# Cosine attention and a highway layer on one core: seven 64-key blocks with quadrant value products, one-piece value loads and stores, folded norm sums, a new order

## The chip, the core and the metric

The kernel runs on one core of one Trainium2 chip. A core has a matrix engine (TensorE, in profiles PE, with its weight loads listed apart as PEld), a vector engine (VectorE, DVE), an activation engine (ScalarE, ACT), a general engine (GpSimd, POOL) and a queue engine (SyncE, SP). SP, POOL and ACT issue the transfers, which 16 DMA engines carry out. TensorE multiplies a stationary operand by a moving one and adds into PSUM, eight banks of 512 float32 columns on 128 partitions. It can be used whole (128 x 128), as two column halves (128 x 64) or as four quadrants (64 x 64); a quadrant is given by the partition half that the operands come from and the partition half of PSUM that the result goes to.

The metric is the time of one execution on the device in microseconds; lower is better. Before the change three runs took 258.66 us (median), 256.27 and 260.71 us.

## What is computed

For 8 batches, 12 heads, 448 positions and 64 numbers per head, queries and keys are scaled to length one, scores are divided by tau = 0.1, and a softmax weights the values. The result, 3584 rows of 768, goes through a highway layer with two 768 x 768 matrices:

```python
q_n = q / (norm(q) + 1e-06);  k_n = k / (norm(k) + 1e-06)
scores = q_n @ k_n.T / tau
attn = exp(scores - max);  attn = attn / (sum(attn) + 1e-09)
x = (attn @ v)            # heads side by side: (3584, 768)
H = maximum(x @ w_h, 0);  T = 1 / (1 + exp(-(x @ w_t + b_t)))
out = T * H + (1 - T) * x
```

Since scores lie between -10 and 10, the kernel leaves the maximum out; the row sums come from a column of ones beside the values.

## The kernel before, in words

**Layout.** A head's 448 positions are split as 64 x 7: partition l holds positions 7l to 7l+6. "Block j" is the 64 positions with remainder j. Two heads of a pair (s = 0, 1) fill 128 partitions, and a group (b, g), i = 3b + g, has four heads: s = 0, 1 and t = 0, 1. There are 24 groups, three to a batch.

**Stages of a batch.** Loads: q on SP in float32, k and v on POOL, converted to 16 bits on the way. v comes in four transfers of 64 partitions (`ld_v`, L370), so that blocks 0 to 2 and 4 to 6, or 0 to 2 and 3 to 5, stand one above the other. `norm` (L402) squares 14 x 64 numbers (mostly ACT, L413; some on POOL or DVE, L415) and DVE sums each 64 of them (L421). A Newton iteration (L432 to L439; for batch 0 logarithm and exponential on ACT, L447 and L450) makes reciprocal lengths, `scale` (L462) multiplies on POOL or DVE, and `turn` puts the number index on the partitions: by PE with a copy out of PSUM on DVE (L474, L482) or by a transposing transfer on SP (L477).

**Attention, batches 1 to 6.** `scores` (L509) makes, for each head pair s, three tiles with 2 x 64 keys above each other for both t (two PSUM banks), and one more tile for the seventh block of all four heads. Every product is a quadrant product, 64 numbers by 64 keys by 448 queries (L316). ACT takes the exponential of each tile of 896 columns into `E` or `Et` (L521, L531), seven per group. `attend` (L535) works on one head pair after its four tiles: 24 full products of 128 keys x 128 queries by 65 value columns (L549) and 8 in column halves for the last 64 queries (L555). The seventh block is paired with zeros in `vp`, so that 128 keys can be used there too. All sums of a pair lie in one bank; DVE takes the reciprocal of the sums (L562) and multiplies (L563).

**Attention, batches 0 and 7.** `attend_tile` (L571) does the same for 128 queries at a time (the last tile 64), so that the highway layer can begin, or end, early (L606, L618, L620, L624, L638 to L643).

**Highway layer.** `ffn` (L648) turns x by a transposing transfer (L672) or PE (L668), multiplies by w_t and w_h (L692; L689 in column halves for the tile of 64 rows), adds the bias on DVE (L721), takes tanh on ACT (L734), makes the gate of it on DVE (L736), and finishes with L730, L757 and L762 (the last on POOL or DVE). The output leaves in two transfers per tile on SP, one per 64 rows (L769 for the short tile, L772 for the others).

**Order.** Every step is an entry ("op") with an engine. `ORDER` is one list of all 1684 ops, written out by hand or by a planner; each engine executes its own ops in that order, and `SLOTS` gives the buffer that each tile takes, among them the eight PSUM banks `B` (score tiles take two neighbouring ones). `ENGINE` moves single ops to another engine than their usual one. For the names in `PORT`, a POOL op is made to wait for the DVE op listed before it; transfers in `HELD` wait for the ACT op listed before them. 18 products on zeros (`wm`, L343) and 41 more (`wf`, L818) fill PE while it has nothing else.

Of the kernel before, what the change touches and what calls it, by code (L numbers as in the profile page):

```python
# [85 lines left out]

SLOTS = {
    "qr": "01010101",
    "kr": "0120121",
    "kn": "012012012120102120210210",  # L90
    "vr": "01010101",
    "vp": "01010101",
# [786 lines left out]
```

## Time and profile before

| | |
|---|---|
| three runs | 258.66 us median, 256.27 to 260.71 |
| the profiled execution: time / span from first to last instruction | 257.48 us / 255.7 us |
| granted TensorE clock | 0.996 of full |
| busy PE / DVE / ACT / POOL | 236.7 / 226.2 / 199.1 / 143.9 us |
| weight loads on PE | 150.0 us |
| DMA packets | 77241, 48.27 MB, 189 GB/s on average |

"Busy" is the union of an engine's instructions. PE's products overlap, and their ends are modelled, so that PE's busy time is more than it needs. Row labels give the line, the engine, the operation, what is written and read, the shape and the count; behind the bar stand the busy time of the group in microseconds, the mean duration of one in nanoseconds, and idle time ahead of it with what ended most of that. A timeline row gives start, length, and the instructions that it gathers. A wait row gives the engine and line that waited, the releaser, the total, the number of waits and the longest.

### The profile page before, as it was taken

What the parts mean: (1) busy time and instruction counts of PE and PEld (TensorE: products, weight loads), DVE (VectorE), ACT (ScalarE), POOL (GpSimd) and SP (SyncE); (2) the same over time, 40 slices, a digit from 0 to 9 for tenths busy, and PEclk for the clock granted to TensorE, in tenths of its full rate; (3) what the DMA queues carried; (4) which work ended last, traced back from release to release, by engine and by line L of the source; (5) the groups of instructions that cost most, each with busy time, mean ns of one, the idle gap of its engine ahead of it and who ended that gap; (6) DMA issues with size and microseconds to landing.
All of it is one profiled execution on the core that took longest, in us unless ns stands there. A gap on an engine that the chain in (4) does not pass through costs nothing.

```text
span 255.7 us, 8889 instructions
## 1 busy us (share of the span) xinstructions
PE 236.7 (93%) x3719; PEld 150.0 (59%) x3719; DVE 226.2 (88%) x509; ACT 199.1 (78%) x248; POOL 143.9 (56%) x172
## 2 busy tenths in 40 slices
PE   5997999999998799999989998899999999999990
PEld 2455675656765466656654654566665766667550
DVE  4869999999997999999997999898998997877894
ACT  3469998999998799999998987699887456875220
POOL 1964879889995769769269731166427221200610
PEclk9999999999999999999999999999999999999998
DMA  6999979999999999998899999999997966992645
GB/s 231 298 229 258 330 126 205 157 151 277 163 147 248 181 211 262 153 161 171 194 242 174 191 153 166 168 316 215 224 144 122 201 145 114 158 165 45 157 141 154
DMA packets 77241, 48.27 MB, mean 189 GB/s; under 512 B 52880, under 2 KB 74000, under 8 KB 77200
## 3 DMA queue, kind: packets, MB, share of 16 engines
q1 hardware_dynamic: 56912, 34.25, 63.2%
q0 software_dynamic: 19856, 12.68, 38.3%
q8 instruction: 29, 0.48, 0.8%
q10 hardware_dynamic: 432, 0.75, 0.8%
q14 instruction: 12, 0.10, 0.1%
HBM read 38.34 MB, written 11.01 MB: 193 GB/s over the span
## 4 chain that ended last, share of the span: by engine, by line
PE 50%; DVE 28%; DMA 9%; ACT 4%; issue 4%; POOL 3%; DVEq 0%; ACTq 0%; POOLq 0%
PE B L692 22%; PE B L316 8%; DMA xT<-x 6%; PE B L549 6%; DVE n L421 5%; PE B L818 3%; DVE hm L730 3%; DVE z L721 3%; DMA vr<-in_v_dram 3%; PE B L689 3%; PE B L343 3%; DVE x L563 2%; PE B L618 2%; ACT E L606 2%; DVE hm L757 2%
## 5 line engine op out<-in xcount | busy, mean ns | idle before, releaser
L521 ACT ACTIVATE E<-B 128x896 f16<-128x896 f32 x108 | 94.3, 923 | 13.8 <-PE B L316 9.5
L692 PEld LDWEIGHTS <-xT 128*128 128x128 f16 x576 | 51.9, 97 | 39.4 <-issue 7.3
L762 POOL TENSOR_TENSOR os<-x,hm 128x384 f32<-128x384 f16 x35 | 31.4, 912 | 56.1 <-DVE hm L757 14.2
L692 PE MATMUL B<-wt,xT 128*128 128x384 f16 x288 | 54.9, 326 | 2.2 <-DMA xT<-x 1.3
L692 PE MATMUL B<-wh,xT 128*128 128x384 f16 x288 | 54.7, 326 | 1.0 <-DMA xT<-x 0.8
L421 DVE TENSOR_REDUCE n<-sq 128x14 f32<-128x896 f32 (+1 forms) x50 | 50.8, 1037 | 2.7 <-ACT sq L413 2.7
L316 PE MATMUL B<-qT,kT 64*64 64x448 f16 (+2 forms) x1064 | 47.9, 283 | 3.5 <-DVE z L721 1.4
L606 ACT ACTIVATE E<-B 128x1024 f16<-128x1024 f32 (+2 forms) x42 | 36.2, 919 | 15.5 <-PE B L316 9.3
L462 POOL TENSOR_TENSOR qn<-qr,y 128x448 f16<-128x448 f32 x38 | 35.2, 936 | 21.0 <-PE B L689 4.1
L462 POOL TENSOR_TENSOR kn<-kr,y 128x448 f16<-128x448 f16 x33 | 30.4, 935 | 17.0 <-DMA kT<-kn 10.5
L549 PEld LDWEIGHTS <-E 128*128 128x128 f16 x648 | 30.4, 98 | 6.9 <-issue 3.6
L734 ACT ACTIVATE tt<-z 128x768 f16<-128x768 f32 (+1 forms) x32 | 24.4, 768 | 12.8 <-DVE z L721 12.7
L549 PE MATMUL B<-vp,E 128*128 128x65 f16 x648 | 33.9, 194 | 0.0
L316 PEld LDWEIGHTS <-kT 64*64 64x64 f16 x1064 | 20.6, 106 | 21.5 <-issue 15.0
L730 DVE SCALAR_TENSOR_TENSOR hm<-B,x 128x384 f16<-128x384 f32 x53 | 28.6, 548 | 4.0 <-PE B L692 2.9
L549 PE MATMUL B<-vp,Et 128*128 128x65 f16 x216 | 30.6, 194 | 0.0
L721 DVE TENSOR_TENSOR z<-B,bias 128x384 f32<-128x384 f32 x48 | 25.6, 549 | 0.9 <-PE B L692 0.5
L563 DVE SCALAR_TENSOR_TENSOR x<-B,rd 128x448 f16<-128x448 f32 x36 | 22.4, 621 | 0.9
L373 POOL DMA_DIRECT2D vr<-in_v_dram x32 | 21.7, 686 | 1.4 <-DVE vp L488 1.1
L549 PEld LDWEIGHTS <-Et 128*128 128x128 f16 x216 | 21.1, 98 | 0.0
L413 ACT ACTIVATE sq<-qr 128x896 f32<-128x896 f32 (+1 forms) x19 | 17.5, 942 | 2.8 <-DMA qr<-in_q_dram 2.8
L531 ACT ACTIVATE Et<-B 128x896 f16<-128x896 f32 x18 | 16.7, 926 | 0.5 <-PE B L316 0.4
(75 smaller groups left out, 307.0 us busy)
## 6 DMA issues: line engine op xcount, KB each, us to landing
out_dram<-os SPq DMA_DIRECT2D x47, 192.0 KB, 3.6
qr<-in_q_dram SPq DMA_DIRECT2D x6, 1344.0 KB, 7.7
kr<-in_k_dram POOLq DMA_DIRECT2D x7, 672.0 KB, 8.1
vr<-in_v_dram POOLq DMA_DIRECT2D x16, 192.0 KB, 6.6
qr<-in_q_dram SPq DMA_DIRECT2D x6, 448.0 KB, 5.8
vr<-in_v_dram POOLq DMA_DIRECT2D x16, 144.0 KB, 7.0
out_dram<-os SPq DMA_DIRECT2D x15, 96.0 KB, 3.5
wt<-in_moe_w_t_dram POOLq DMA_DIRECT2D x1, 1152.0 KB, 13.2
```

The costliest lines, as they stand in the source:

```text
L316: nc.tensor.matmul(out, lhsT=tokens("k", i, s, j, 1, ln), rhs=tokens("q", i, s, j0, n, ln), start=True, stop=True)
L421: nc.vector.reduce_sum(R("n2", b)[:, c : c + 7 * n], a, axis=AX.X)
L462: ENG[eng].tensor_mul(R(nm + "n", i)[:, :, t, :], source(nm, b, g)[:, t, :].rearrange("l (j d) -> l j d", d=D), R("y", b)[:, c : c + 7].un ...
L521: op("ACT", f"exd {n} {c}", lambda c=c, at=at, n=n: nc.scalar.activation(R("E", n)[:, 14 * c : 14 * c + 14, :].rearrange("l (t j) x -> l t ...
L549: nc.tensor.matmul(U_()[:, 2 * c + t, :], lhsT=keys(t, m, 2 * c, 2), rhs=values(b, g, s, t, m), start=(m == 0), stop=(m == NC))
L563: op("DVE", f"ev {n}", lambda: nc.vector.scalar_tensor_tensor(out=R("x", b)[:, :, D * p : D * p + D], in0=U_()[:, :, 0:D], scalar=0.0, in1 ...
L606: op("ACT", f"ex{m} {n}", lambda at_=at_, m=m, o=o: nc.scalar.activation(flat()[:, o : o + 2 * m].rearrange("l (t x) -> l t x", t=2), R2(a ...
L692: nc.tensor.matmul(P[:, 0:MH], lhsT=xT[:, cc, :], rhs=w_[:, cc, MH * mh : MH * mh + MH], start=(cc == 0), stop=(cc == CC - 1))
L721: op("DVE", f"za {g} {mh}", lambda at=at, sl=sl: nc.vector.tensor_add(R("z", g)[:, sl], R("B", at)[:, 0:MH], biast[:, :] if tail else bias ...
L730: op("DVE", f"hm {g} {mh}", lambda at=at, sl=sl, mh=mh: nc.vector.scalar_tensor_tensor(out=R("hm", g)[:, sl], in0=R("B", at)[:, 0:MH], sca ...
L734: op("ACT", f"th{nb} {g}", lambda: nc.scalar.activation(R("tt", g)[:, 0:W], R("z", g)[:, 0:W], AF.Tanh, scale=0.5), r=[("z", g), ("t0",)], ...
L762: op(eng, f"out {g} {mh}", lambda sl=sl, mh=mh, eng=eng: ENG[eng].tensor_add(R("os", g)[:, sl], xpart(mh), R("hm", g)[:, sl]), r=[("gg", g ...
```

## The change

- **Scores.** Each score tile now holds one 64-key block j of all four heads of a group: head pair s on the partition half s, t in the bank. Seven tiles of 896 columns as before; no tile of its own for a seventh block. `E` becomes 11 tiles of 1024 columns, `Et` goes.
- **Value products.** They use 64 keys and 64 queries each, in quadrants; part j of a group runs after exponential j and adds to sums of all four heads in a bank pair. 196 products per group. The zero padding of the values goes. One reciprocal (14 columns) and one multiplication (896 columns) finish a group.
- **Values.** One transfer per batch in k's layout; two copies per batch into `vp` (DVE, in three cases ACT and in one POOL); the separate copies of the seventh block go. The ones are set on POOL.
- **Norm sums.** For 42 of the 48 (q or k, batch, group) a fold first adds the upper 32 squares of each 64 to the lower 32, on POOL (23) or DVE (19); DVE then sums 32.
- **Stores.** One transfer per tile but for the last two tiles.
- **Engines.** 12 of the 32 gates move from DVE to ACT; of the 96 half-tile scalings 40 instead of 22 are on DVE, of the 53 output sums 30 instead of 18. Squares: 39 instead of 37 pairs on ACT, 3 instead of 2 on DVE, 4 instead of 7 on POOL.
- **Batch 0's keys** land in the buffers of the weights, which are loaded after they have been read.
- **Fillers.** 45 `wf`, no `wm`.
- **Order and slots** are new throughout, 1600 ops. The ACT queue's own transfers no longer count as the ACT op that held transfers wait for.

```diff
-NF = 41
+NF = 45
+FOLD = {('q', 3, 2), ('q', 6, 1), ('k', 5, 0), ...
...
-        op("DVE", f"zvp {i}", zero("DVE", [(t[:, :, :, 0:3, D : D + 1], 1.0), (t[:, :, :, 3, 0 : D + 1], 0.0)]
+        op("POOL", f"zvp {i}", zero("POOL", [(t[:, :, :, D : D + 1], 1.0)]), w=[("zvp",)])
...
     def ld_v(b):
-        for s, jj, j0, n in ((0, 0, 0, 4), (0, 1, 4, 3), (1, 0, 0, 3), (1, 1, 3, 4)):
...
+        op("POOL", f"ldv {b}", lambda: nc.gpsimd.dma_start(R("vr", b)[:, :, :], q_src(v, b)), w=[("vr", b)])
...
+            fold = i in FOLD
+            if fold:
+                eng = pick(f"fd{n} {nm} {b} {g} {t}", "POOL")
+
+                def ff_(eng=eng, a=a):
+                    A = R("sq", i)[a].rearrange("l (g d) -> l g d", d=D)
+                    ENG[eng].tensor_add(A[:, :, 0:32], A[:, :, 0:32], A[:, :, 32:64])
...
+                nc.vector.reduce_sum(R("n2", b)[:, c : c + 7 * n], A[:, :, 0:32] if fold else A, axis=AX.X)
...
     def scores(b, g):
         i = 3 * b + g
+        for j in range(NJ):
+            at = ("D", i, j)
+
+            def fn(j=j, at=at):
+                for s in range(2):
+                    for t in range(2):
+                        product(R2(at)[64 * s : 64 * s + 64, 512 * t : 512 * t + S], i, s, j, 0, NJ, t)
...
+    def attend(b, g):
...
+        def U_():
+            return R2(at).rearrange("l (s x) -> l s x", s=2)[:, :, 0:455].rearrange("l s (g e) -> l s g e", e=65)
...
+        for j in range(NJ):
+            def part(j=j):
+                X, stop = U_(), j == NJ - 1
+                for c in range(NC):
+                    for t in range(2):
+                        for s in range(2):
+                            for h in range(2):
+                                nc.tensor.matmul(X[64 * h : 64 * h + 64, s, 2 * c + t], lhsT=E_(s, j, t, 2 * c + h, 1),
+                                                 rhs=values(b, g, s, t, j), start=(j == c == t == 0), stop=False)
+                for s in range(2):
+                    for t in range(2):
+                        nc.tensor.matmul(X[64 * t : 64 * t + 64, s, 6], lhsT=E_(s, j, t, 6, 1), rhs=values(b, g, s, t, j),
+                                         start=False, stop=stop)
...
+        op("DVE", f"rc {i}", lambda: nc.vector.reciprocal(R("rd", i)[:, :, :], U_()[:, :, :, D]), r=[("B", at)], w=[("rd", i)])
+        op("DVE", f"ev {i}", lambda: nc.vector.tensor_mul(
+            R("x", b)[:, :, 128 * g : 128 * g + 128].rearrange("p j (s d) -> p s j d", s=2), U_()[:, :, :, 0:D],
...
+        parts = (((0, 4), (4, 7)) if i < 3 else ((0, 7),))
...
+        u = ("D", "V", I, i)
...
+                eng = pick(f"gt{nb} {g}", "DVE")
...
+                    if eng == "ACT":
+                        nc.scalar.activation(t_, t_, AF.Copy, scale=0.5, bias=0.5)
...
-                for h in range(2):
-                    nc.sync.dma_start(rows[2 * i + h], O[64 * h : 64 * h + 64, :])
+                nc.sync.dma_start(rows[2 * i : 2 * i + 2], O[:, :])
...
-                if o.eng == "ACT":
+                if o.eng == "ACT" and not o.name.startswith(("ld", "sl")):
```

More of the change, by code (lines that the diff above doesn't have):

```diff
@@ L480, in turn @@
             return
-        op("PE", f"t{nm} {b} {g}", fn, r=rd + [("id",)] + ([("wm",)] if i == 0 and nm == "k" else []), w=[("B", at)], mode="F")
-        op("DVE", f"cp{nm} {b} {g}", lambda: nc.vector.tensor_copy(
-            turned(nm, i), R16(at)[:, 0:896].rearrange("p (s x) -> p s x", s=2)), r=[("B", at)], w=[tn(nm, i)])
+        op("PE", f"t{nm} {b} {g}", fn, r=rd + [("id",)], w=[("B", at)], mode="F")
+        copy(f"cp{nm} {b} {g}", lambda: turned(nm, i), lambda: R16(at)[:, 0:896].rearrange("p (s x) -> p s x", s=2),
+             r=[("B", at)], w=[tn(nm, i)])
@@ L524, in scores @@
-        at = ("D", "t", i)
-        def ft():
-            for s in range(2):
-                for t in range(2):
-                    product(R2(at)[64 * s : 64 * s + 64, 512 * t : 512 * t + S], i, s, 3 + 3 * s, 0, NJ, t)
-        op("PE", f"qkt {i}", ft, r=[tn("q", i), tn("k", i)], w=[("B", at)], mode="T")
-        op("ACT", f"exdt {i}", lambda: nc.scalar.activation(
-            R("Et", i).rearrange("l (t j) x -> l t (j x)", t=2),
-            R2(at).rearrange("l (t x) -> l t x", t=2)[:, :, 0:S], AF.Exp, scale=1.0 / tau), r=[("B", at)], w=[("Et", i)])
@@ L537, in attend @@
+    def attend(b, g):
         i = 3 * b + g
+        at = ("D", "U", i)
         def U_():
-            return R("B", ("U", n))[:, 0:455].rearrange("p (g e) -> p g e", e=65)
-        def keys(t, m, j, w):
-            X, at = (R("E", n), 7 * (2 * m + t) + j) if m < NC else (R("Et", i), 7 * t + j)
-            return X[:, at : at + w, :].rearrange("l j x -> l (j x)")
-        def full(c):
-            for t in range(2):
-                for m in range(NC + 1):
-                    nc.tensor.matmul(U_()[:, 2 * c + t, :], lhsT=keys(t, m, 2 * c, 2), rhs=values(b, g, s, t, m),
-                                     start=(m == 0), stop=(m == NC))
@@ L552, in tail @@
-        def tail():
-            for m in range(NC + 1):
-                for t in range(2):
-                    nc.tensor.matmul(U_()[64 * t : 64 * t + 64, 6, :], lhsT=keys(t, m, 6, 1), rhs=values(b, g, s, t, m),
-                                     start=(m == 0), stop=(m == NC))
-        rd = [("E", n), ("Et", i), ("vp", b, s), ("vp", b, s, "t")]
-        for c in range(NC):
-            op("PE", f"av {n} {c}", lambda c=c: full(c), r=rd, w=[("B", ("U", n))], mode="F")
-        op("PE", f"avt {n}", tail, r=rd, w=[("B", ("U", n))], mode="C")
@@ L600, in fq, with E_ @@
+        def E_(s, j, t, h):
+            n = 0 if i == 3 or j < 4 else 1
+            j0, j1 = parts[n]
+            o = ((j1 - j0) * t + j - j0) * w + 64 * h
+            return R("E", e + (n,))[64 * s : 64 * s + 64, o : o + 64]
+        for n, (j0, j1) in enumerate(parts):
+            at_, m = ("D", "0", I, i, n), (j1 - j0) * w
+            def fq(j0=j0, j1=j1, at_=at_):
+                for j in range(j0, j1):
                     for s in range(2):
                         for t in range(2):
-                            product(T[64 * s : 64 * s + 64, 512 * t + 384 : 512 * t + 384 + w], I, s, 3 + 3 * s, 2 * i, nq, t)
@@ new lines, in fq @@
+                            o = 512 * t + w * (j - j0)
+                            product(R2(at_)[64 * s : 64 * s + 64, o : o + w], I, s, j, 2 * i, nq, t)
+            op("PE", f"qk{m} {I} {i} {n}", fq, r=[tn("q", I), tn("k", I)], w=[("B", at_)], mode="T")
+            op("ACT", f"ex{m} {I} {i} {n}", lambda at_=at_, m=m, n=n: nc.scalar.activation(
+                R("E", e + (n,))[:, 0 : 2 * m].rearrange("l (t x) -> l t x", t=2), R2(at_).rearrange("l (t x) -> l t x", t=2)[:, :, 0:m],
+                AF.Exp, scale=1.0 / tau), r=[("B", at_)], w=[("E", e + (n,))])
@@ new lines, in attend_tile, with av @@
+        u = ("D", "V", I, i)
+        nt = 2 if i < 3 else 1
+        def U_():
+            return R2(u).rearrange("p (s x) -> p s x", s=2)[:, :, 0 : 65 * nt].rearrange("p s (t e) -> p s t e", e=65)
+        def av():
+            X = U_()
+            for j in range(NJ):
+                for t in range(2):
+                    for s in range(2):
+                        for h in range(nt):
+                            o = X[64 * h : 64 * h + 64, s, t] if i < 3 else X[64 * t : 64 * t + 64, s, 0]
+                            nc.tensor.matmul(o, lhsT=E_(s, j, t, h), rhs=values(b, g, s, t, j),
+                                             start=(j == 0 and (t == 0 or i == 3)), stop=(j == NJ - 1 and (t == 1 or i == 3)))
@@ L648, in ffn @@
+        op("DVE", f"{'ev0' if i < 3 else 'evt0'} {I} {i}", ev, r=[("B", u), ("rd", ("q", I, i))], w=[("x", b, i)])
     def ffn(b, i):
@@ L735, in ffn, with gate @@
                    r=[("z", g), ("t0",)], w=[("tt", g)])
-                op("DVE", f"gt{nb} {g}", lambda: nc.vector.tensor_scalar(
-                    out=R("tt", g)[:, 0:W], in0=R("tt", g)[:, 0:W], scalar1=0.5, scalar2=0.5, op0=ALU.mult, op1=ALU.add),
-                   r=[("tt", g)], w=[("gt", g)], u=[("tt", g)])
+                eng = pick(f"gt{nb} {g}", "DVE")
+                def gate(eng=eng):
+                    t_ = R("tt", g)[:, 0:W]
+                    if eng == "ACT":
+                        nc.scalar.activation(t_, t_, AF.Copy, scale=0.5, bias=0.5)
+                    else:
+                        ENG[eng].tensor_scalar(out=t_, in0=t_, scalar1=0.5, scalar2=0.5, op0=ALU.mult, op1=ALU.add)
+                op(eng, f"gt{nb} {g}", gate, r=[("tt", g)], w=[("gt", g)], u=[("tt", g)])
                 if late:
```

260 lines of the change are left out of this document (96 added, 164 removed), and 123 rows, old and new, of the table ORDER.

## The prediction

> **What bounds the kernel now.** I read the page's busy line first, then busy time by stretch, then who waits in the long middle, then the chain. The stretches cut where the work changes: up to about 40 us batch 0 is attended tile by tile, at 200 us the last wide score exponential of batch 6 has just ended, and from 233 us only the gate layer is left.
>
> ```profile
> span 255.7 us, 8889 instructions
> PE 236.7 (93%) x3719; PEld 150.0 (59%) x3719; DVE 226.2 (88%) x509; ACT 199.1 (78%) x248; POOL 143.9 (56%) x172
> ...
> PE 50%; DVE 28%; DMA 9%; ACT 4%; issue 4%; POOL 3%; DVEq 0%; ACTq 0%; POOLq 0%
> ```
>
> ```profile
> 0.00:40.00 40.00, 34.52 (x575) 21.29 (x575) 31.97 (x77) 29.09 (x40) 25.51 (x34) 1.00 1.01 244
> 40.00:200.00 160.00, 152.93 (x2278) 95.56 (x2275) 150.05 (x324) 144.39 (x177) 107.01 (x127) 1.00 1.16 192
> 200.00:233.00 33.00, 32.94 (x717) 23.19 (x715) 27.27 (x68) 20.73 (x27) 5.98 (x7) 1.00 0.81 142
> 233.00:256.00 23.00, 16.28 (x166) 9.97 (x162) 16.89 (x42) 4.89 (x7) 5.39 (x6) 0.95 0.51 134
> ```
>
> The columns after the length are PE, weight loads, DVE, ACT, POOL, then TensorE clock, DMA share, GB/s. In the 160 us middle DVE is busy 150.05 us (94%), ACT 144.39 (90%) and PE 152.93, which overstates PE since the ends of its products are modelled. From 200 to 233 us PE alone is full (32.94 of 33). The chain gives PE half the span, but three engines are nearly even, so the waits of the middle decide whether a saving on one of them can count:
>
> ```profile
> DVE rd L562 <- PE B L549: 2.0, 2, 1.4
> DVE vp L488 <- DMA vr<-in_v_dram: 1.5, 1, 1.5
> ...
> ACT E L521 <- PE B L316: 9.5, 14, 1.6
> ```
>
> Between 40 and 200 us, DVE's named waits add up to 6.8 us, the first two rows being the largest; its other 3 us are gaps between instructions. ACT's 9.5 us wait for scores is a wait for an engine that was itself waiting or full. So **DVE sets the pace of the middle, PE that of 200 to 233 us**, and dependences that of the two ends.
>
> **PE.** Rows for the value products before, and for the nearest thing to a quadrant value product, the 64x64 score products of the last query tile:
>
> ```profile
> L549 PE MATMUL B<-vp,E 128*128 128x65 f16 x648 | 33.9, 194 | 0.0
> 231.02 0.54 PE L618 MATMUL B<-vp,E 128*128 128x65 f16 x12
> 231.49 0.64 PE L316 MATMUL B<-qT,kT 64*64 64x64 f16 x56
> ...
> 120.19 0.65 PE L692 MATMUL B<-wh,xT 128*128 128x384 f16 x3
> 120.77 0.86 PE L316 MATMUL B<-qT,kT 64*64 64x448 f16 x12
> ```
>
> Twelve full products take 0.54 us; without the 0.194 us of the last, eleven starts are 0.0315 us apart. Fifty-six quadrant products take 0.64 us; without one duration of 0.19 us, their 14 sets of four are 0.032 us apart. So four quadrant products cost one full product. By the code a head group (four heads) has 48 full products and 16 in column pairs, 56 slots, for its values; after, 196 quadrant products, 49 slots. Over 24 groups that is 1344 x 0.0315 = 42.3 us against 1176 x 0.032 = 37.6 us: **-4.7 us**. Upper bound: no overlap at all, 4704 x 0.0315 = 148 us, +106; the row next to it has the same tile, 64 instead of 65 columns, so I take it.
>
> The Trainium skill speaks against this edit: TensorE: Matmul & The Clock Gate, section "Wait — 56ns, not 53.3ns?", says that starts of products never come closer than about 25 ns. By that floor the 4704 products would take an estimated 118 us instead of 37.6. Here 56 start within 0.45 us, 8 ns each, so this trace does not show the floor for products in different quadrants.
>
> A change of tile shape costs too: the third L692 product ends at 120.84 and so began 0.326 us before (its row's mean), at 120.51; its followers are 0.162 apart, yet L316 starts 0.26 later: 0.095 us. In the two lists I count 180 such changes before and 153 after: **-2.6 us**. Fillers (products on zeros) fall from 59 to 45, in the head only, where they cover waits: nothing.
>
> **DVE.**
>
> ```profile
> L421 DVE TENSOR_REDUCE n<-sq 128x14 f32<-128x896 f32 x46 | 48.5, 1074 | 0.5 <-ACT sq L413 0.5
> L421 DVE TENSOR_REDUCE n<-sq 128x7 f32<-128x448 f32 x4 | 2.3, 614 | 2.3 <-ACT sq L413 2.2
> L462 DVE TENSOR_TENSOR qn<-qr,y 128x448 f16<-128x448 f32 x10 | 6.2, 618 | 1.3 <-ACT y L450 1.3
> L563 DVE SCALAR_TENSOR_TENSOR x<-B,rd 128x448 f16<-128x448 f32 x36 | 22.4, 621 | 0.9
> L624 DVE SCALAR_TENSOR_TENSOR x<-B,rd 128x256 f16<-128x256 f32 x18 | 7.6, 424 | 0.6
> L562 DVE RECIPROCAL rd<-B 128x7 f32<-128x7 f32 x36 | 6.9, 195 | 3.0 <-PE B L549 2.0 <-ACT E L521 0.7 <-PE B L555 0.2
> L488 DVE COPY vp<-vr 128x1152 f16<-128x1152 f16 x16 | 7.4, 470 | 1.5 <-DMA vr<-in_v_dram 1.5
> L498 DVE COPY vp<-vr 64x384 f16<-64x384 f16 x7 | 2.1, 303 | 0.1
> L736 DVE TENSOR_SCALAR tt<-tt 128x768 f16<-128x768 f16 x24 | 9.6, 409 | 1.3 <-ACT tt L734 1.3
> L762 DVE TENSOR_TENSOR os<-x,hm 128x384 f32<-128x384 f16 x18 | 9.7, 552 | 0.3
> ```
>
> - Folded sums: 42 reductions of 896 become reductions of 448, 42 x (1.074 - 0.614) = -19.3; 19 of the 42 folds (adds of 448) are on DVE at 0.618 = +11.7. Together -7.6. A fold reads 32 of every 64 numbers; the nearest rows are contiguous, and if the stride cost half as much again the folds would give 5.9 back.
> - Evictions: 36 x 0.621 become 18 of 896 numbers. From 256 to 448 numbers the time grows by 0.197, so 896 take 0.621 + 448 x 0.197/192 = 1.08: 22.4 to 19.4, -3.0. Reciprocals 36 x 0.195 to 18 of 14, some 0.244: -2.6.
> - Value copies: 16 x 0.470 + 7 x 0.303 = 9.6 to 12 x 0.470 x 1344/1152 = 6.6: -3.0.
> - Gates: 12 of 32 go to ACT, 8 x 0.409 and 4 small ones (0.279): -4.4. Memsets to POOL: -1.9, all before the first data.
> - Moved from POOL: 18 scalings at 0.618, 12 output sums at 0.552, one more square: +18.8.
>
> In all **-3.7 us** of 226.2. It matters where. I add the durations along the two lists, each of the longer ones shortened by 0.08 us, since the next instruction starts that much early:
>
> ```profile
> 85.53 2.07 DVE L421 TENSOR_REDUCE n<-sq 128x14 f32<-128x896 f32 x2
> ```
>
> (two of 1.074 us in 2.07). The cuts are the second activation-table load, the last wide exponential of batch 6, and the end:
>
> | us | DVE | PE | ACT |
> |---|---|---|---|
> | to the table load | 33.8 to 25.9 | 29.2 to 18.9 | 28.4 to 28.4 |
> | middle | 149.9 to 156.1 | 141.5 to 145.0 | 141.2 to 148.5 |
> | rest | 45.4 to 40.2 | 51.2 to 48.4 | 24.2 to 30.1 |
>
> The before column for DVE in the middle (149.9) agrees with the 150.05 measured. So the new order carries DVE work out of the head into the very stretch that DVE bounds.
>
> **ACT.**
>
> ```profile
> L521 ACT ACTIVATE E<-B 128x896 f16<-128x896 f32 x108 | 94.3, 923 | 13.8 <-PE B L316 9.5 <-DVE hm L757 1.3 <-PE B L549 1.1
> L734 ACT ACTIVATE tt<-z 128x768 f16<-128x768 f32 x24 | 20.3, 848 | 9.0 <-DVE z L721 8.8
> L734 ACT ACTIVATE tt<-z 128x384 f16<-128x384 f32 x8 | 4.2, 527 | 3.8 <-DVE z L721 3.8
> ```
>
> Exponentials stay 126 of 896. Added: 8 gates at 0.848 and 4 at 0.527 (nearest: tanh of the same size) 8.9, three value copies, at 0.923 x 1344/896 = 1.4 each 4.2, two squares 1.9: **+15 us**, half of it after the middle, where ACT stands idle. In the middle ACT goes from 88% to 93%: hidden, unless DVE gets faster than I think.
>
> **POOL, queues, transfers.**
>
> ```profile
> L462 POOL TENSOR_TENSOR qn<-qr,y 128x448 f16<-128x448 f32 x38 | 35.2, 936 | 21.0 <-PE B L689 4.1 <-DVE y L439 2.8 <-issue 2.5
> L373 POOL DMA_DIRECT2D vr<-in_v_dram x32 | 21.7, 686 | 1.4 <-DVE vp L488 1.1 <-POOL vp L498 0.3
> L358 POOL DMA_DIRECT2D kr<-in_k_dram x7 | 6.3, 894 | 4.7 <-DMA E<-in_k_dram 4.7
> ...
> vr<-in_v_dram POOLq DMA_DIRECT2D x16, 192.0 KB, 6.6
> wt<-in_moe_w_t_dram POOLq DMA_DIRECT2D x1, 1152.0 KB, 13.2
> ```
>
> POOL loses 18 scalings, 12 sums (each about 0.92), 9 small copies, 3 squares and 24 value-load issues (32 x 0.686 to 8 x 0.894, the key load's issue, which has the new shape): 28 us less after adding 23 folds. POOL was 44% idle, so nothing by itself, but value loads no longer stand between its sums, and the 1.5 us wait of DVE for a value transfer goes. Stores go from 60 issues on SP to 30; a transposing transfer of x stands in the same queue. Batch 0's keys now land in the weight buffers, so the first weight load is issued after five scalings more, near 18 us, and lands near 31; its first product in the list stands behind the table load. That cover is some 5 us; without it PE waits.
>
> **The sum** against the profiled execution: 255.7 us span and 1.8 us around it, 257.48; the runs' median is 258.66 (256.27 to 260.71), so it is an ordinary one.
>
> ```profile
> 18.07 0.78 ACT E L606
> ```
>
> ```profile
> DVE x L482 <- PE B L474: 1.9, 2, 1.1
> ```
>
> - Head: the first exponential starts at 18.07, after the two copies of batch 0's turned q and k have waited 1.9 us for PE, which waits for halves scaled one after another on POOL. The list now scales both halves of the first k tile on DVE while POOL scales those of q, so the two copies follow each other some 3 us earlier: first exponential about 15.3. ACT's list from there to the table load holds the same 18.7 to 19.6 us. **-2.7** (0 to -3.3).
> - Middle: DVE +6.2; of its 6.8 us of waits I take away 4.7: the value transfer (1.5), the wait for value products (2.0; they now follow each exponential, and only the last seventh is late) and 1.2 of PE's. **+1.5** (-0.6 to +6.2).
> - Rest: PE-bound, 51.2 to 48.4: **-2.8** (-1 to -5, gates on ACT shorten the last chain).
>
> -4.0 us: span 251.7, time **253.5 us**. The terms' ends, all on one side, would give 248.6 and 262.7.
>
> **Rivals.**
> 1. *DVE's work in the middle is paid in full* (+6.2 less the 1.5 of the value transfer, head -2.0, rest -2.8): -0.1, 257.4. For it: 94% busy already. Against: 5.3 us of other waits to win back. Chance 0.20.
> 2. *PE sets the end everywhere*: -4.7 - 2.6 - 2.7 from the head: 247.5. For it: half the chain is PE. Against: DVE with 156 us of work in some 160. Chance 0.22.
> 3. *Slower: two-bank sums starve the exponentials.* A group's accumulator now holds two of eight PSUM banks from its first value part until one 1.08 us eviction, before one bank per head. In the lists the next scores stand ahead of the running exponential for 41 of 126 before, for 15 after. Where PE is late, ACT waits, and DVE behind it. If each of 18 groups loses one exponential's 0.92 us, +16.6; if half do, +8.3: 262 to 270. It decides once ACT's wait for scores passes 9.5 + 10 us. Chance 0.13.
> 4. *Quadrants don't overlap as claimed* with accumulation into one bank pair: even a third of the 106 us gives 290. Chance 0.02.
>
> **How the numbers follow.** Forecast 0.43, rivals as above. About 2% (5.2 us of 258.66, so 253.5) is what a measurement of this kernel can tell from no change, and the forecast lies on that edge: half of it and rival 2 give faster 0.44, the other half and rival 1 same 0.41, rivals 3 and 4 slower 0.15. Range 246.5 to 260.5: from 1 us below rival 2 to 3 us above rival 1, the part of the middle's upper end (+6.2) and the head's (0) that can come together; rivals 3 and 4 and the tails of the forecast are left out.
>
> **What would show it.** Right: 4704 quadrant value products with sets of four 0.032 us apart; reductions of 0.61; evictions near 1.08; first exponential near 15.3; DVE busy about 222 and 95% or more of the middle; POOL near 115; ACT near 214. Wrong: DVE with long waits for PE or ACT in the middle (rival 3), folds well over 0.62, or ACT busier than DVE, which would make my bound the wrong engine.

## The result

The changed kernel takes **448.54 us** (median of 4 runs, 447.45 to 453.98) against 258.94 us for the kernel before in the same comparison (256.27 to 260.71): a ratio of 1.742, 95% interval 1.720 to 1.765. The forecast was 253.5 us. Executions of one kernel fall into a faster and a slower state (in one job the kernel before took 255.9 to 267.5 us, at granted clocks of 0.996 to 0.969); the times below are medians of the fast runs of each job.

The page of the profiled execution after the change: span and busy times, the granted clock in 40 slices, the instruction queue of the DMA part (number of packets, MB, share of 16 engines), and the chain that ended last by engine.

```profile
span 452.0 us, 15134 instructions
...
PE 277.8 (61%) x6873; PEld 165.1 (37%) x6873; DVE 229.6 (51%) x492; ACT 215.9 (48%) x265; POOL 120.4 (27%) x132
...
PEclk9966699879886997989757588996578769758575
...
q8 instruction: 53, 0.87, 0.9%
...
PE 40%; DMA 25%; issue 22%; DVE 7%; SPq 3%; ACT 2%; POOL 0%; DVEq 0%; POOLq 0%; ACTq 0%
```

The work outside PE hardly grew: DVE has 229.6 us instead of 226.2, ACT 215.9 instead of 199.1, POOL 120.4 instead of 143.9. PE shows 277.8 us instead of 236.7, part of it at a lower clock. All the engines are idle for longer: none is above 61%. The chain shows two things that the chain before had little of, "DMA" (25% of 452 us, 113 us; before 9% of 256, 23 us) and "issue" (22%, 99 us; before 4%, 10 us), which is time in which an engine, here mostly TensorE, stood still and waited for nothing that the profile knows. The granted TensorE clock falls to 0.5 to 0.8 in many slices, where it was full nearly throughout.

Busy time by stretch (PE, weight loads, DVE, ACT, POOL, then clock, DMA share, GB/s). In the middle that the prediction took from DVE's 94%, DVE now has 63%:

```profile
40.00:200.00 160.00, 114.75 (x3096) 68.17 (x3096) 101.53 (x217) 99.32 (x119) 62.30 (x65) 0.84 0.79 114
200.00:400.00 200.00, 119.99 (x3084) 72.25 (x3083) 85.89 (x187) 84.92 (x104) 37.68 (x39) 0.77 0.80 90
```

The waits (engine, line, whom it waits for: us in all, times, longest):

```profile
ACT E L520 <- PE B L320: 108.4, 38, 16.1
...
PEld L541 <- issue: 52.1, 24, 6.8
PE B L541 <- issue: 48.1, 14, 6.7
...
DVE os L726 <- DMA out_dram<-os: 35.5, 9, 8.5
```

ScalarE waits 108.4 us for score products (before: 9.5). Two kinds of wait stand behind this, and neither is in the prediction.

**TensorE stops where many short products stand together** (the value products of L541 above all), up to 8.5 us at a time, with all semaphores satisfied. Count TensorE's instructions in the trace, a weight load and a product being two: of the 34 stops of more than 1 us, measured from the end of one product to the start of the next, 26 fall at the same place in a block of 256 instructions. They add up to 99 us, as much as the chain's "issue". The other eight (44 us) end with a transfer or with another engine's work. The kernel before has three stops of more than 1 us, 3.9 us in all, and none of them at that place. The instruction queue moves packets of 16,384 bytes, 53 of them where the kernel before has 29:

```profile
q8 instruction: 29, 0.48, 0.8%
```

TensorE's 13,746 and 7,438 instructions are 53.7 and 29.1 blocks of 256. After 21 of the 26 stops TensorE goes on 1.3 to 1.6 us after such a packet has landed. So one packet is the next block of 256 instructions, and where short products stand together, a block is used up before the next has been fetched.

**Output rows wait for their buffer** until an earlier store has left. In the last part the DMA moves little but stores, and its share tells how many of the 16 engines they use:

```profile
420.00:428.00 8.00, 5.28 (x23) 2.44 (x24) 2.52 (x5) 0.00 (x0) 0.00 (x0) 0.50 0.13 52
```

A share of 0.13 is 2 engines of 16, at 52 GB/s; a store of 384 KB then takes 384 x 1024 / 52 = 7.5 us. In the packet records a one-piece store's 128 packets of 3,072 bytes take 7.5 to some 10 us with two in flight; in the kernel before, the same 128 packets take 1.8 to 2.8 us where little else is in the way, with 6 to 14 in flight. The Trainium skill states the rule in DMA: Bandwidth & Descriptors, section "Why a DMA increments its semaphore by 16 and not by 1": a transfer runs on the largest number of engines, up to 16, that divides the slowest dimension of both its sides. The DRAM side of the new store is 2 x 64 x 768, so that would be two engines; the trace agrees with its 0.13.

### The profile page after: what moved, and what is told of

It reads as the page before. It is cut to its first block, busy times and chain, and to the rows that moved or that the text cites. A ratio compares the mean times of both kernels' runs of the same rounds, so it can differ in the third digit from the quotient of the medians.

```text
span 452.0 us, 15134 instructions
## 1 busy us (share of the span) xinstructions
PE 277.8 (61%) x6873; PEld 165.1 (37%) x6873; DVE 229.6 (51%) x492; ACT 215.9 (48%) x265; POOL 120.4 (27%) x132
## 4 chain that ended last, share of the span: by engine, by line
PE 40%; DMA 25%; issue 22%; DVE 7%; SPq 3%; ACT 2%; POOL 0%; DVEq 0%; POOLq 0%; ACTq 0%
PE B L650 16%; DMA out_dram<-os 15%; PE B L320 8%; PE B L541 6%; DMA xT<-x 4%; PE B L647 4%; DMA qT<-qn 3%; DMA qr<-in_q_dram 3%; PE B L593 3%; SPq L630 2%; PE B L490 2%; DVE n L426 1%; PE B L545 1%; ACT E L577 1%; DVE z L679 1%
## 5 line engine op out<-in xcount | busy, mean ns | idle before, releaser
L520 ACT ACTIVATE E<-B 128x896 f16<-128x896 f32 x126 | 109.7, 920 | 110.6 <-PE B L320 108.4
L320 PE MATMUL B<-qT,kT 64*64 64x448 f16 (+2 forms) x1064 | 64.0, 326 | 33.2 <-issue 19.4
L541 PE MATMUL B<-vp,E 64*64 64x65 f16 x3024 | 46.1, 206 | 48.1 <-issue 48.1
L650 PE MATMUL B<-wh,xT 128*128 128x384 f16 x288 | 67.0, 378 | 8.1 <-DVE hm L688 5.5
L541 PEld LDWEIGHTS <-E 64*64 64x64 f16 x3024 | 42.6, 117 | 55.6 <-issue 52.1
L692 ACT ACTIVATE tt<-z 128x768 f16<-128x768 f32 (+1 forms) x32 | 24.3, 763 | 45.3 <-DVE z L679 44.2
L420 POOL TENSOR_TENSOR sq<-sq 128x448 f32<-128x448 f32 x23 | 25.7, 1128 | 58.9 <-ACT sq L408 23.2
L647 PE MATMUL B<-wt,xT 128*64 128x384 f16 x96 | 13.8, 415 | 35.5 <-DMA xT<-x 20.6
L545 PE MATMUL B<-vp,E 64*64 64x65 f16 x504 | 30.9, 206 | 7.3 <-issue 7.3
L726 DVE TENSOR_TENSOR os<-x,hm 128x384 f32<-128x384 f16 x30 | 16.1, 553 | 35.7 <-DMA out_dram<-os 35.5
L426 DVE TENSOR_REDUCE n<-sq 128x14 f32<-128x448 f32 (+2 forms) x50 | 31.2, 648 | 1.2 <-POOL sq L420 0.6
L647 PEld LDWEIGHTS <-xT 128*64 128x64 f16 x180 | 11.2, 133 | 45.1 <-DMA xT<-x 21.2
```

Source lines behind the costliest of these rows:

```text
L320: nc.tensor.matmul(out, lhsT=tokens("k", i, s, j, 1, ln), rhs=tokens("q", i, s, j0, n, ln), start=True, stop=True)
L426: nc.vector.reduce_sum(R("n2", b)[:, c : c + 7 * n], A[:, :, 0:32] if fold else A, axis=AX.X)
L520: op("ACT", f"exd {i} {j}", lambda j=j, at=at: nc.scalar.activation(R("E", (i, j))[:, 0:896].rearrange("l (t x) -> l t x", t=2), R2(at).re ...
L541: nc.tensor.matmul(X[64 * h : 64 * h + 64, s, 2 * c + t], lhsT=E_(s, j, t, 2 * c + h, 1), rhs=values(b, g, s, t, j), start=(j == c == t == ...
L545: nc.tensor.matmul(X[64 * t : 64 * t + 64, s, 6], lhsT=E_(s, j, t, 6, 1), rhs=values(b, g, s, t, j), start=False, stop=stop)
L647: nc.tensor.matmul(P[64 * h : 64 * h + 64, 0:MH], lhsT=xT[:, cc % 3, 64 * (cc // 3) : 64 * (cc // 3) + 64], rhs=w_[:, cc, MH * h : MH * h ...
```

## The experiments

Two theories: **F**, TensorE's instructions are fetched too slowly for the many short products; **S**, one-piece stores run on two DMA engines and hold up what shares these. The rival is the prediction's own third case, **P**: value sums of two banks, or the new order, starve the exponentials by themselves. Each job ran the kernel before on the same chip too; its time there stands beside each result, and differences are taken from it.

| kernel | us | kernel before, same job | ratio, 95% |
|---|---|---|---|
| changed kernel | 448.5 | 258.9 | 1.742 (1.720 to 1.765) |
| changed, value products 128 queries wide | 415.2 | 264.8 | 1.569 (1.553 to 1.585) |
| changed, stores by columns | 431.5 | 257.2 | one run |
| changed, two-piece stores | 329.0 | 264.8 | 1.244 (1.224 to 1.263) |
| ... and wide value products | 284.9 | 257.2 | 1.111 (1.076 to 1.145) |
| ... and 5073 products | 281.3 | 255.9 | 1.099 (1.079 to 1.119) |
| ... and 3873 products | 265.7 | 259.7 | 1.017 (1.006 to 1.029) |
| before, one-piece stores | 400.1 | 257.2 | 1.560 (1.544 to 1.577) |
| before, the same from GpSimd's queue | 382.2 | 255.9 | 1.494 (1.487 to 1.501) |
| before, score products cut in four | 276.5 | 264.8 | 1.045 (1.028 to 1.062) |
| before, 1024 quadrant products at the end | 289.6 | 264.8 | one run |

### Wider value products

```diff
-for h in range(2):
-    nc.tensor.matmul(X[64 * h : 64 * h + 64, s, 2 * c + t], lhsT=E_(s, j, t, 2 * c + h, 1), ...)
+nc.tensor.matmul(X[:, s, 2 * c + t], lhsT=E_(s, j, t, 2 * c, 2), ...)
```

(in batches 0 and 7 likewise)

> The changed kernel with its value products 128 queries wide (64 keys x 128 queries, two of them side by side instead of four quadrants): the same arithmetic in the same 49 slots a group, but PE has some 9,700 instructions instead of 13,700. Theory F (PE runs out of instructions: it stops at every 256th one when a block of 256 is executed in less than about 3.5 us): most stops go, 250 to 300 us. Theory S (the one-piece stores and the queue they stand in): nothing changes, 440 us or more. Theory P (the two-bank sums leave the exponentials without banks): nothing changes, 440 us or more.

415.2 us, outside the ranges of all three theories: three tenths fewer instructions bring back only 33 us of the 190 lost (39 measured from the kernel before in each job). The stops at block ends are all but gone, one of 1.8 us instead of 26 with 99 us. But 17 other stops of more than 1 us now make 94 us, and nine of these, 67 us, end with a transposing transfer of q, k or x. So the two kinds of wait lay partly side by side: what the instructions no longer hold up, the transfers do, and this run by itself can't price F.

### Two-piece stores

```diff
-nc.sync.dma_start(rows[2 * i : 2 * i + 2], O[:, :])
+for h in range(2):
+    nc.sync.dma_start(rows[2 * i + h], O[64 * h : 64 * h + 64, :])
```

(the tail's store likewise)

> The changed kernel with the stores in two pieces as before. S: the waits for stores (35.5 us on DVE, 30.5 us on POOL, 15% of the chain) go, 380 us or less. F and P: within 2% of the changed kernel, 440 to 457 us.

329.0 us: 120 us come back from this edit alone (125 measured from the kernel before in each job). Its waits:

```profile
ACT E L520 <- PE B L320: 51.2, 30, 4.6
...
PEld L541 <- issue: 26.1, 15, 4.4
```

No wait for a store or a transposed tile is among the long ones any more. The stops of TensorE remain, 21 of the 23 over 1 us at block ends, but shorter: 1.2 to 4.6 us, 55 us in all. (The 65 us in an expectation below count from the start of the last product, and all 24 stops that this gives.) One-piece stores can lengthen a fetch too: in the changed kernel one packet of instructions took 7.3 us, from 249.3 us on, while a one-piece store was under way from 247.7 to 255.2; here none takes over 1.8 us.

### One-piece stores in the kernel before

```diff
-for h in range(2):
-    nc.sync.dma_start(rows[2 * i + h], O[64 * h : 64 * h + 64, :])
+nc.sync.dma_start(rows[2 * i : 2 * i + 2], O[:, :])
```

> The kernel before with one edit: each of the 30 early stores as one transfer whose DRAM side is 2 x 64 x 768, as in the changed kernel. If such a store takes 7.5 us or more instead of 1.8 to 2.8 and holds up what is queued behind it whatever the kernel (transposing transfers of x, instruction fetches), 275 to 310 us, and the waits for the stores and for the transposed x appear. If the store only hurts where TensorE is already short of instructions, 257 to 268 us: this kernel has half as many instructions. If the number of transfers is what counts, within 2% of before or faster (30 issues fewer on the queue).

400.1 us, far above the expected 275 to 310: this one edit costs the kernel before 143 us (400.1 - 257.2; the 137 in the next expectation is from the median of all seven runs of the kernel before, 262.7). Its chain, which can be followed back only to 195 us and so covers the second half of the span, and its waits:

```profile
DMA 30%; PE 11%; DVE 2%; issue 2%; SPq 1%; ACT 1%; POOL 0%; DVEq 0%; ACTq 0%
...
DMA xT<-x 12%; DMA qT<-qn 10%; DMA out_dram<-os 7%; PE B L692 5%; PE B L316 2%; PE B L689 2%; PE B L618 1%; DMA qr<-in_q_dram 1%; SPq L770 1%; SPq L477 0%; ACT E L521 0%; DVE hm L730 0%; PE B L555 0%; PE B L549 0%; POOL qn L462 0%
```

```profile
POOL os L762 <- DMA out_dram<-os: 48.6, 7, 10.1
...
PE B L316 <- DMA qT<-qn: 42.2, 4, 20.5
...
PEld L692 <- DMA xT<-x: 32.5, 6, 10.4
```

The store does its damage less by itself than through what waits beside it: the transposing transfers of q and x. In the timeline, SP issues three stores at 86.7, and then the issue of two transposes takes 19.50 us by itself; the score products that need them begin after 20.5 us of waiting:

```profile
86.68 8.64 SPq L770 DMA_DIRECT2D out_dram<-os  x3
95.44 19.50 SPq L477 DMA_TRANSPOSE qT<-qn  x2
```

```profile
117.12 1.33 PE L316 MATMUL B<-qT,kT 64*64 64x448 f16 x12 [20.50 <-DMA qT<-qn]
```

I had expected less because I took a store as 7.5 us against 2.8 and not as a queue of several: 23 stores of 384 KB at 7.5 us and 7 of half that size make an estimated 200 us of two engines in a kernel of 257, and three of them can come at once.

### The queue or the engines

Here the same one-piece stores are issued by GpSimd instead of SP (`nc.gpsimd.dma_start`, the operation moved to POOL's list at the same place).

> The kernel before with one-piece stores as in the 400 us run, but issued by GpSimd, so that they stand in another queue than the transposing transfers of q, k and x. If those transfers lose their time because they stand behind a store in the same queue, most of the 137 us comes back: 265 to 300 us, with the waits for transposed q, k and x gone (GpSimd itself is held up where a store waits for its sums, some us). If the two DMA engines that a store keeps busy are what holds them, whichever queue it came from, 370 to 420 us with the same waits.

382.2 us, in the range of the second theory. The stores no longer stand in the queue of the transposes, and the score products still wait for these:

```profile
PE B L316 <- DMA qT<-qn: 30.8, 4, 10.4
```

What the transposes and the stores still share is the DMA engines. The transposes of x land later, though their queue holds no store until the end; median time from issue to landing in the kernel before and, in the second line, here:

```profile
xT<-x SPq DMA_TRANSPOSE x28, 4.1
```

```profile
xT<-x SPq DMA_TRANSPOSE x28, 9.4
```

How much of the 126 us that makes isn't shown, since GpSimd now also waits 46.6 us at its stores for VectorE's work. Time from the issue of a store to its landing, here and, in the second line, in the kernel before:

```profile
DMA to landing us min/median/max: 7.1/13.5/23.8
```

```profile
DMA to landing us min/median/max: 2.1/3.5/9.5
```

### Two transfers, but cut by columns

```diff
-nc.sync.dma_start(rows[2 * i : 2 * i + 2], O[:, :])
+for n in range(2):
+    nc.sync.dma_start(rows[2 * i : 2 * i + 2, :, MH * n : MH * n + MH], O[:, MH * n : MH * n + MH])
```

> The changed kernel with each store in two transfers again, but cut by columns: each of the two has a DRAM side of 2 x 64 x 384. If it is the outer count of 2 that leaves a store to two DMA engines, the stores stay long (two of 3.7 us or more one behind the other) and the time stays near the changed kernel's, 420 to 455 us; if the two transfers fall on different engines, in between, 350 to 400 us. If what counts is one transfer against two, the time is that of the two-piece stores, 322 to 336 us.

431.5 us (one run), as expected from the outer count. So it isn't one transfer against two: two transfers of 2 x 64 x 384 stay slow, two of 64 x 768 are fast. In a stretch with little but stores the share is again about two engines of 16 (0.14):

```profile
400.00:408.00 8.00, 5.22 (x42) 2.62 (x38) 2.93 (x6) 1.05 (x2) 0.91 (x1) 0.80 0.14 52
```

### Instruction supply measured by itself

The kernel before, with 1024 quadrant products on zeros behind its last work:

```diff
+for m in range(1024):
+    t, h = m // 2 % 2, m % 2
+    nc.tensor.matmul(BALL[64 * h : 64 * h + 64, 512 * t : 512 * t + 64], lhsT=wz[64 * t : 64 * t + 64, 0:64],
+                     rhs=wz[64 * t : 64 * t + 64, 128:192], start=True, stop=True)
```

> The kernel before with 1,024 more quadrant products of 64 columns on zeros after everything else, when no transfer of size is under way: the price of instruction supply by itself. F: eight blocks of 256 instructions at 3.3 us or more each, 26 us or more from the first to the last, span 275 to 290 us. If instructions are not the limit (the 8 ns a product that the trace of before shows for 56 of them): 8 us from first to last, span 260 to 266 us.

289.6 us, 25 more than before. The timeline of TensorE, start and length of each run of products:

```profile
264.19 1.24 PE L846 MATMUL B<-wz 64*64 64x64 f16 x128 [2.61 <-issue]
267.91 1.92 PE L846 MATMUL B<-wz 64*64 64x64 f16 x128 [2.49 <-issue]
271.37 1.92 PE L846 MATMUL B<-wz 64*64 64x64 f16 x128 [1.53 <-issue]
275.10 1.93 PE L846 MATMUL B<-wz 64*64 64x64 f16 x128 [1.81 <-issue]
278.55 1.93 PE L846 MATMUL B<-wz 64*64 64x64 f16 x128 [1.53 <-issue]
```

Exactly 128 products at a time, with their 128 weight loads a block of 256 instructions, and from one block to the next 3.45 to 4.0 us, though the DMA is nearly idle (a share of 0.07). The products of a block need 1.2 to 1.9 us. The packet records show where the rest goes: the packet of the next block starts 1.1 us after the block ahead of it has begun, takes 0.9 to 1.4 us, and TensorE goes on 1.2 to 1.5 us after it has landed. So in a steady stream 256 TensorE instructions take at least some 3.5 us here, however short they are. The Trainium skill, in Runtime: NRT & Kernel Launch, section "Instruction fetch mechanics", says that instructions come in 16 KiB blocks of 256 and that crossing into the next is mostly hidden. The block size agrees with the trace; that it is hidden agrees with the kernel before, whose shortest block runs 4.3 us and where nothing stops at a block's end, but not with these products.

### More instructions in the kernel before

The wide score products of the kernel before, each cut into four along the queries (3719 products become 5231).

> The kernel before with each wide score product cut in four (128, 128, 128 and 64 queries): the same columns, but 1,512 products and as many weight loads more, 10,460 PE instructions instead of 7,440. Layout, order, banks and stores are those of before. F: a new loss of 20 to 100 us, with stops of over 1 us at every 256th PE instruction. S and P: only some 2.5 ns for each set of four more, 1 us, so 259 to 262 us, and no such stops.

276.5 us, +11.7: less than F's 20 to 100, and well more than the 1 us of the others. There are six stops at block ends, 12 us in all, that the kernel before does not have, for instance

```profile
163.38 0.41 PE L318 MATMUL B<-qT,kT 64*64 64x128 f16 x12
166.90 0.78 PE L318 MATMUL B<-qT,kT 64*64 64x128 f16 x36 [3.11 <-issue]
```

The blocks ahead of these stops ran for 4.4 to 5.8 us, so such blocks can stop as well; what made their fetches late isn't shown. The stops are as large as the loss.

### Both causes taken back

Two-piece stores and wide value products together.

> The changed kernel with both suspected causes taken back at once: value products of 64 keys by 128 queries (4857 products instead of 6873) and stores in two pieces of 64 partitions. If instruction supply of TensorE and one-piece stores are together the whole loss, 260 to 285 us: the kernel before has 3719 products and no stops, and cutting its score products up to 5231 cost 11.7 us. If the two causes only add (33 us from the wide products, 120 us from the stores), 449 - 33 - 120 = about 296 us. If value sums that hold two banks starve the exponentials by themselves, or the new order is at fault, more than 300 us, with ScalarE still waiting over 40 us for the score products and with few stops of TensorE at every 256th instruction.

284.9 us, at the upper end of the first case (260 to 285) and 28 us above the kernel before. Five stops of more than 1 us are left, 8.8 us, two of them at block ends (3.2 us). But the wide product has a price of its own: TensorE is busy 262.7 of 287.8 us, and by the starts in the trace its value products take 65 us where those of the kernel before take 50. So the run takes back F, adds some 15 us of TensorE's work, and separates less than I hoped: some 13 us stay open.

### The quadrant form with fewer products

In these two runs the stores are in two pieces and the value products keep their quadrant form, but part of them is left out, as the expectations say.

```diff
-for c in range(NC):
+for c in range(0 if j % 2 else NC):
...
-for j in range(NJ):
+for j in range(0, NJ, 2):
```

> The changed kernel with two-piece stores and with part of the value products left out, all in their quadrant form: of the key blocks 1, 3 and 5 only the products of the last query block are kept (in batches 0 and 7 none), so the attention output lacks those keys; 5073 products instead of 6873, every other instruction as it was. The value products alone, without stops, take some 48 us in the two-piece run, so leaving out 1800 of 4704 takes at most 18 us of TensorE's own work: 329 - 18 = 311 us if TensorE's work, the two-bank sums or the new order make the loss. If instruction supply makes it, the stops at every 256th instruction (65 us in the two-piece run) mostly go as well and the exponentials' wait for score products falls from 51 us to under 30: 260 to 280 us.

281.3 us, just above the 260 to 280 of instruction supply: 25 us over the kernel before where the run with all products lay 64 over. Of these 39 us TensorE's own work accounts for at most 18. The exponentials' wait falls from 51.2 to

```profile
ACT E L520 <- PE B L320: 21.4, 21, 2.7
```

Eight stops remain at block ends, 17 us.

```diff
-for c in range(0 if j % 2 else NC):
+for c in range(NC if j in (0, NJ - 1) else 0):
...
-for j in range(0, NJ, 2):
+for j in (0, NJ - 1):
```

> The changed kernel with two-piece stores and with still more value products left out: of the key blocks 1 to 5 only those of the last query block (in batches 0 and 7 none), so the attention output lacks those keys; 3873 products, about as many as the kernel before has, every other instruction as in the changed kernel. TensorE's own work falls by some 30 us against the whole set and no block of 256 instructions should run out early. What is left is what the rest of the change costs on VectorE, ScalarE and GpSimd: 250 to 259 us if the rest is harmless (VectorE's pace, as in the prediction's first two cases); 262 to 275 us if value sums of two banks or the new order starve the exponentials by themselves. If the remaining 20 us of the run with 5073 products were not instruction supply, the time stays at 275 to 282 us.

265.7 us, ratio 1.017 (1.006 to 1.029). That lies in the range set for P (262 to 275) and above that for a harmless rest. But no stop at a block's end is left, and the sign of P is absent: the exponentials' wait, which P would have had to lengthen, is as in the kernel before (9.5):

```profile
ACT E L520 <- PE B L320: 9.1, 15, 1.3
```

```profile
40.00:200.00 160.00, 137.26 (x2442) 76.08 (x2432) 148.76 (x315) 148.07 (x182) 88.67 (x92) 1.00 1.06 185
```

The two-bank sums are all there in this run (the same 18 groups, the same evictions), so **P is not the cause of the bulk**: 6 us (2 to 7 by the interval) are left for everything else in the change, against the 190 lost. Where these few come from stays open. VectorE and ScalarE, both at 93% of the middle, are the fullest engines. The run has some 27 us less of TensorE's work than the two-piece run (by the starts in the traces, 21.7 us of value products for 48.3) and still isn't faster than before. That P would cost nothing with all the products there isn't shown, and what the change would be worth with all its products and free instruction supply stays open too.

## Why the prediction was wrong

- **Failed: "Stores go from 60 issues on SP to 30", costed at nothing.** I counted issues and not the engines that a transfer uses. The price is 120 us (448.5 to 329.0, taking it back) or 143 us (putting it alone into the kernel before). That "a transposing transfer of x stands in the same queue" was seen as a gain; what the transposes share with the stores is the engines, and with one-piece stores in the kernel before a score product waited 20.5 us for them. The rule by which it could have been seen stands in the page of the Trainium skill named above, and the DRAM side's 2 x 64 x 768 stands in the diff.
- **Failed: the value products, -4.7 us.** Their rate holds only in a burst. In the changed kernel 24 + 4 products follow each other every 0.22 to 0.24 us, 0.031 to 0.034 us per set of four, close to the 0.032 taken from the row of 56:

```profile
203.87 0.38 PE L541 MATMUL B<-vp,E 64*64 64x65 f16 x24
204.08 0.20 PE L545 MATMUL B<-vp,E 64*64 64x65 f16 x4
204.11 0.36 PE L541 MATMUL B<-vp,E 64*64 64x65 f16 x24
204.30 0.21 PE L545 MATMUL B<-vp,E 64*64 64x65 f16 x4
204.33 0.38 PE L541 MATMUL B<-vp,E 64*64 64x65 f16 x24
```

  But 56 products are 112 instructions, less than half a block. Where such products go on beyond a block, the supply sets the rate: 3.45 us for 32 sets, 0.108 us each. (On average it would suffice: by an estimate 53.7 blocks at 3.45 us are 185 us, less than any span here. The stops come where short products stand together.) The step that failed is to carry a burst's rate over to 4704 products, with no term for their instructions; the page of the kernel before showed 29 instruction packets and no gap that would price them. The floor of 25 ns that the prediction cites from the Trainium skill's TensorE: Matmul & The Clock Gate does not show here either: 128 quadrant products in 1.24 us are less than 10 ns each. Even without stops the saving was not there: by the starts in the trace, leaving out gaps over 0.4 us, the value products take 50.2 us before and after (48.3 with two-piece stores), at a lower clock.
- **DVE's total: -3.7 forecast, +3.4 measured** (226.2 to 229.6). The mis-sized term is the value copies:

```profile
L420 POOL TENSOR_TENSOR sq<-sq 128x448 f32<-128x448 f32 x23 | 25.7, 1128 | 58.9 <-ACT sq L408 23.2 <-DVE sq L420 17.8 <-DVE sq L410 14.8
L426 DVE TENSOR_REDUCE n<-sq 128x14 f32<-128x448 f32 x42 | 24.8, 610 | 0.9 <-POOL sq L420 0.6
L550 DVE TENSOR_TENSOR x<-B,rd 128x896 f16<-128x896 f32 x18 | 19.6, 1089 | 0.5
L420 DVE TENSOR_TENSOR sq<-sq 128x448 f32<-128x448 f32 x19 | 11.9, 638 | 2.2 <-ACT sq L408 2.2
L480 DVE COPY vp<-vr 128x1344 f16<-128x1344 f16 x12 | 10.1, 845 | 0.0
```

  Reductions (0.610 for 0.614), evictions (1.089 for 1.08) and folds (0.638 for 0.618, so the stride costs almost nothing) were right. The value copies take 0.845 us for 0.55, 3.5 us in all: the price per number was carried over from a copy of another layout. With that the durations added up should come out even, and they do: 253.5 us before, 253.8 after. The other 3 us are overlap: busy time counts once where one instruction starts before the last has ended, and that happens less often on an engine that keeps waiting. A fold on POOL takes 1.128 us, more than the scalings' 0.93, which accounts for most of POOL's 120.4 for 115; ACT's 215.9 for 214 was right.
- **The bound.** "DVE sets the pace of the middle" was right for the kernel before, and in the run with 3873 products DVE is back at 148.8 of 160 us. In the changed kernel DVE is idle for more than a third of the middle. The sign to look for that I had named, DVE with long waits for PE, did appear, but not for the reason of the third rival.
- **The head**: the first exponential starts at 16.34 us, 1.7 us earlier than before and not 2.7; right in kind, and lost in the rest.

```profile
16.34 1.00 ACT L577 ACTIVATE E<-B 128x1024 f16<-128x1024 f32 x1
```

- **Rivals.** The first was added up with -2.0 for the head where its own term is -2.7; with that it is 256.7 and not 257.4. The third gave 262 to 270 us for what ScalarE's wait would cost; the wait came (108 us), but most of its cause lies in TensorE's stops and the transfers. The fourth had a price of the right order, 290 us and more, for a mechanism that did not occur: the quadrants do overlap. No case held a transfer that becomes slower by being joined, nor the supply of instructions. The two causes together, from the kernel before in each job: of 190 us, 125 go with the stores, and of the remaining 64, 58 go when the products are cut to 3873; up to 27 of these 58 can be TensorE's own work. The causes overlap, as the wide products showed, so these shares hold for this order of taking them back.
- The change of tile shapes (-2.6) and the late weight load (some 5 us of cover) can't be read among stops of this size.

## What to carry to other kernels

Before joining two transfers, write down the slowest dimension of both sides: the joined one can run on as few DMA engines as that count, and whatever else uses those engines, transposes and instruction fetches included, waits behind it. Two causes that lie side by side can hide each other: taking back one alone may show little. Count TensorE's instructions as well as its slots: where 256 of them (128 products with their weight loads) run in less than about 3.5 us for more than one block, the fetch sets the pace, and a rate read from a burst shorter than a block says nothing about it. When all engines get idler at once and "issue" grows in the chain, look at what feeds them and not at their work.

## What was not expected of the hardware

- In a stream of short products 256 TensorE instructions took no less than 3.45 us from block to block with nearly idle DMA; beside one-piece stores a single stop at a block's end took up to 8.5 us.
- A leading 2 is not slow as such. The loads of q have the same 2 x 64 rows, but there the two steps join into 128 equally spaced rows (64 x 448 numbers are just the step of the leading dimension), and in the packet records of the kernel before 11 to 16 of their packets are in flight, at 216 GB/s or more. In the store the leading step (768) and the row step (7 x 768) don't join. That this is why is argued from the shapes, not tested.
- An idle TensorE also came with a lower clock, whatever it was waiting for: the mean granted clock was 0.996 with PE busy for 93% (before), 0.885 with 78% (two-piece stores), 0.833 with 65% (one-piece stores in the kernel before, with one stop at a block's end) and 0.788 with 61% (changed kernel). It isn't in strict order everywhere: with wide products and two-piece stores it was 0.945 at 91%. The mean of a gate-layer product went from 326 ns (L692 before) to 378 for one matrix and 359 for the other:

```profile
L650 PE MATMUL B<-wh,xT 128*128 128x384 f16 x288 | 67.0, 378 | 8.1 <-DVE hm L688 5.5 <-issue 2.5 <-DVE z L679 0.2
```
